# Moving the loads around a gated SSM and linear-attention kernel: a weight's halves on two queues, B in eight quarter loads

## The chip, the cores and the metric

The kernel runs on one core of one Trainium2 chip. The core has five engines that work side by side, each through its own list of instructions in program order: PE (TensorE, the matmuls; its weight loads are shown apart as PEld), DVE (VectorE), ACT (ScalarE), POOL (GpSimd) and SP (SyncE), which computes nothing and issues most of the DMA transfers. The metric is the device time of one execution in microseconds (us); less is better.

## The reference

Everything is bfloat16, S = 2048 rows of D = 512. A state-space branch and a linear-attention branch are mixed by a gate of the row:

```python
g = sigmoid((x * gate_w).sum(-1, keepdims=True))

# branch a: diagonal complex state space, 512 states
dt = exp(log_dt); Lam_bar = exp(dt * Lam)
B_bar = ((Lam_bar - 1) / Lam)[:, None] * (B_re + 1j * B_im)
Bu = einsum("bld,pd->blp", x, B_bar)
h[t] = Lam_bar * h[t-1] + Bu[t]                 # over 2048 steps
a = 2 * einsum("blp,dp->bld", h, C_re + 1j * C_im).real + x * Dskip

# branch b: linear attention, 32 heads of 16
q, k, v = split(x @ wqkv)                       # the input x is A_x
pq, pk = q @ w_phi, k @ w_phi                   # for each head
phi_q = concat(softmax(pq), softmax(-pq));  phi_k = the same of pk
kv = phi_k^T v;  z = sum of phi_k over the rows
o = (phi_q kv) / (phi_q z + 1e-6)
b = o @ wo

out = g * a + (1 - g) * b
```

## The kernel before

The 2048 rows are 16 tiles of 128 rows, x tile 0 to 15, each brought in transposed by one DMA (`x_load`, line 229). The work is cut into stages, Python generators that issue a few instructions and stop at each `yield`. The string `ORDER` (lines 24 to 52) is a list of tokens written out by hand; the loop at line 804 takes each token and moves the stage of that name on by one step. So `ORDER` is the program order of every engine, and of SP's queue too: each engine works off its own part of it, strictly in that order. `@3` names a PSUM bank, `:D` puts an evacuation on DVE in place of ACT, and `F:28` issues 28 filler matmuls on a constant tile.

The stages that the change touches or that follow from it:

- **The key weight.** K's weight (512 x 512, tile `C2r`, line 162) comes in two halves of 256 rows. `W0` to `W3` (line 271) transpose its four row tiles on PE; W0 and W1 read the first half, W2 and W3 the second. `B` (line 342) builds a block diagonal of `w_phi` on DVE from the tile `Wc`. `f0` to `f3` (the folds, line 428) multiply the two on PE and write the folded weight `Wk2`, the evacuations partly on ACT and partly on DVE. `k0` to `k15` (line 478) then multiply an x tile with all of `Wk2`, four matmuls each; `v0` to `v15` do the same with V's weight `Wv`.
- **Small vectors.** POOL loads three vectors of the state space into `vec_n` and two others into `vec_m`. `V` (line 308) transposes `vec_n` on PE and copies it out on DVE; the stages `P`, `P2` and on compute the recurrence's coefficients from it.
- **B.** `NR` and `NI` (line 283) load the real and the imaginary half of B into the tile `Bn`: the real rows in partitions 0 to 63, the imaginary ones in 64 to 127, eight groups of 64 states, t = 0 to 7, along the free dimension. `R0` to `R7` (line 287) transpose one group t of `Bn` into `BT` by DMA. `g` + r + j (line 596) multiplies x with the two groups t = 2j and 2j + 1 of `BT`, four matmuls each, in this order: so g00, g60, g20, g10, g30 and g40 need R0 and R1, g41 is the first that needs R2 and R3, and g23 the first that needs R6.
- **Other DMAs in SP's order.** `l8` to `l15` load x tiles 8 to 15. `C0` to `C7` and `Q0` to `Q3` (lines 295, 291) bring C and Q's weight in transposed; `J0` to `J3` (line 299) rearrange C into the tiles `X1` and `X2`; `O` loads the last weight.

SP's own order before is: `Wc`; x tiles 0 to 3; `Wv`; x tiles 4 to 7; NR; NI; x tiles 10, 13, 9, 12, 14, 11, 8; R0; R1; x tile 15; R2; C4; R3; C6; C3; Q3; Q2; Q1; C7; Q0; C0; R4; C2; R5; C1; C5; six transfers of J; R7; two of J; R6; O. The two halves of K's weight go out on ACT's queue.

The functions that the change touches:

Of the kernel before, what the change touches and what calls it, by code (L numbers as in the profile page):

```python
# [23 lines left out]
ORDER = """
NR F:28 NI B W1@0 W0@1 W0 W2@2 W1:D W3@3 W3 f1@4 W2:D f0@5 f2@6 f0 f1:D l10 V@0 F:4 V P f3@1 f3 f2:D F:4 P P k1@2 k1
l13 P2 k0@3 P2 U P2 P2 P2 P2 P4 k2@4 P3 P3 k3@5 P4 P4 k0 v0@0 i0 i2 U i0 i0 i1 i2 k4@7 i0:D i0 k2 i2 i2:D i2 U k3 k5@6
i1 v3@1 n0 x0 l9 i1 V2@2 i3 l12 x0 k4 v2@3 i3 i3 l14 i1 k5 n0 x0 n0 x0 i3 k7@4 n0 x0 U n0 i1 l11 k6@5 n1 x1 x1 n1 x1
n1 l8 R0 R1 x1 i3 k7 M v7@7 x1 n1 n1 k6:D L V2 v1@6 x2 n2 e0 v6@4 v5@5 v4@2 e0 x2 s0 v0 l15 n2 s0 n2 v2 s0 v1 R2 s0 v6
v3 n2 k10@0 k10 s0 k9@3 k9 C4 k13@6 gw D R3 s0 k12@4 e1 v7 s0 e1 s1 C6 k11@1 k11 x2 s1 k14@0 k8@3 k12 k14 k8 v4 k13
a0@71 a0 x2 s1 x2 s1 v5 g00@4 g00 g60@0 n2 x3 s1 g20@3 g60 s1 g10@2 g10 n3 e2 g30@6 g40@5 g10 s1 a1 x3 g20 n3 a1 x3 n3  # L30
x3 g41@4 n3 C3 e2 e2 e2 x3 g30 g40 g30 k15@0 k15 n3 e3 s2 x4 s2 x4 g01@2 g01 e3 e3 s2 g50@3 g11@5 g50 s2 s2 s2 n4 x4
n4 Q3 n4 s2 g50 g21@6 e3 s3 v8@0 g31@2 g11 Q2 g11 n4 g70@3 Q1 s3 C7 g21 g70 v9@5 g70 g70 z0 z0 g31 g31 Q0 w1@6 C0 a2
a2 a2 w0@3 s3 z0 v11@2 v9 g61@5 g41 R4 z0 w1 v8 z0 z0 g61 s3 w2@4 s3 s3 a2 x4 z0 z0 g51@6 g51 x4 w2 C2 s3 w3@0 g51 v11
n4 R5 w3 g71@5 g71 g71 g71 z1 z1 g02@4 g02 g42@6 a3 a3 z0 z0 g42 w0 e4 e4 z1 z1 z1 g62@2 g12@0 q1@5 C1 h50@4 C5 J1 e4
e4 z1 q2@6 q2 g12 g12 g22@3 g22 J0 h50 z1 z1 g62 q3@4 q3 J2 s4 z1 s4 q0@6 z1 s4 q0 q1 xA nA g32@0 J3 g32 g32 h60@3 J0
g52@2 g52 c4 h60 J2 c4 g52 h51@4 c2 s4 s4 g72@6 R7 g72 xA h10@5 nA g72 g72 c2 xA J3 nA h10 v10@0 v10 J1 s4 c5 h51 c5
R6 g23@3 v12@2 c4 c0 c0 g63@5 nA z2 z2 a3 a3 g03@4 xA g03 z2 z2 z2 z2 xA g23 z2 z2 g33@6 c5 v12 z2 z2 g13@0 g13 g63
g43@4 h32@3 g13 nA g43 h52@2 h52 g33 h32 h61@5 h61 h12@0 c0 g53@4 h12 g33 g53 s4 v14@3 c2 eA eA h42@2 h42 g73@6 g53 eA
eA g73 g73 q10@5 sA h11@0 h11 O h00@4 g73 sA v13@2 h00 v13 a4 z3 sA v15@6 z3 v15 h20@0 h01@4 h30@2 v14 h20 sA h30 z3
h31@6 z3 z3 sA a4 h01 h31 c6 c6 sA q13@3 q13 z3 a4 a4 Y Y h22@0 G q10 z3 z3 G q6@2 q6 h22 z3 z3 sA sA Y Y c1 c1 q9@4  # L40
q8@6 q5@7 h62@3 h41@5 c3 h41 c1 c3 c3 h13@0 h62 q11@2 h13 q11 q8 q12@1 c6 q12 h21@5 q5 h21 h02@2 c7 q4@6 q4 h53@3 h53
h23@1 h23 h33@0 h33 sA q9 h40@7 h40 sA q7@5 h43@6 h63@3 c7 h43 q7 c7 y4@0 y4 sA h63 sA h03@1 END h02 o0@4 o0 X1 N1
o1@7 o1 q14@6 X1 N1 h03 o0@5 X1 o1@2 o1 o1 o0 o0 q15@3 o2@4 o2 o2@7 o2 N1 q15 X1 N1 X1 N1 E1 E1 y2@1 y1@2 y1 E1 E1 q14
X2 y0@5 y0 o1 y4 X2 N2 X2 o0 o0 o3@4 o3 o3@7 o3 o1 o3 y2 X2 N2 o2 X2 N2 S1 S1 N2 S1 o3 S1 N2 S1 S1 o3 y5@3 o2 o2 S1 S1
S1 y1 E2 E2 E2 E2 y9@6 G N3 y5 y5 y3@4 y2 X3 X3 N3 t1 G t1 N3 S1 N3 S2 y9 y9 S2 S2 S1 S1 S2 y3 y3 t3 y0 t0 t0 t2 t2
y6@7 X3 t2:A o4@2 o4 o4@5 o4 o4 y6 y6 t3 X3 o4 X3 o4 S2 S2 t3 o5@1 o5 o5@2 o5 o5 y13@5 y13 o5 N3 o6@4 S2 o6 o6@1 o6 o6
y12@2 o5 y7@4 y7 y12 o6 o6 t4 y7 S2 S2 t4:D S2 E3 E3 E3 E3 S2 o7@1 o7 t5 t5 S3 o7@0 o7 S3 o7 t6 S3 o7 S2 o7 y8@1 o8@3
t6 o8 o8@0 o8 o8 S3 S3 y12 t0:A y11@7 o8 o8 o9@3 o9:D o9@0 o9:D S3 y8 y8 o9 o9 S3 S3 o9 o10@3 y11 o10 o10@0 y11 o10
o10 S3 y14@3 S3 y14 t7 t7:D t8 y14 t8 y15@0 o11@4 S3 o11 o11@1 t9 o12@4 o11:D o11 S3 o10 o10 o12 o12@1 o12 o12 t9:D
o11 y15 o13@4 o13:D o13@6 t6:A o13 o13 o11 o12 y10@1 o14@4 y15 o14:D o12@6 t9 o12:D t7:A t1 y10 y10 o13 o15@4 o15  # L50
o15@6 t4:A t5 o15 o15 t8 o15 t12 t12 t12:A t10 o14@4 o14 o14 t10:D o13@6 t11 o15@2 o15 t10 o13:D t11 t11:A y13 t13 o14
o14@1 t15 t15 t15 o14:D t14 t13 t13 t14 t14:A
"""
# [15 lines left out]
def kernel(  # L69
# [91 lines left out]
    Wv = const.tile([P, KT, D], BF16, name="Wv")  # L161
    wk_nat = const.tile([P, KT, D], BF16, name="C2r")
    C2r = wk_nat
    for k0 in (0, 2):
        nc.scalar.dma_start(out=wk_nat[:, k0:k0 + 2, :], in_=B_wqkv[k0 * P:(k0 + 2) * P, D:2 * D].rearrange("(k p) n -> p k n", p=P))
    nc.sync.dma_start(out=Wc[:], in_=B_w_phi.rearrange("(k hl) e f -> (hl e) k f", hl=8))
# [71 lines left out]
    nc.sync.dma_start(out=Wv[:], in_=B_wqkv[:, 2 * D:3 * D].rearrange("(k p) n -> p k n", p=P))
    for ti in range(4, 8):
        x_load(ti)  # L240
    fk_g = tc.tile_pool(name="featK", bufs=3, reuse_waits="tile")
    fk = fk_g.__enter__()
# [37 lines left out]
        x_load(ti)  # L280
        yield

    def st_N(ri):
        nc.sync.dma_start(out=Bn[ri * 64:(ri + 1) * 64, :, :], in_=(A_B_re, A_B_im)[ri].rearrange("(t p) d -> p t d", p=64))  # L284
        yield

    def st_BT(t):
        nc.sync.dma_start_transpose(out=BT[:, :, t, :], in_=Bn[:, t, :])
# [559 lines left out]
```

## Time and profile before

| what | value |
|---|---|
| time, median of 3 runs | 155.53 us (155.44 to 155.6) |
| span of the profiled execution | 153.2 us |
| busy on PE | 146.2 us, 95% of the span |
| busy on DVE, ACT, POOL | 132.4, 129.2 and 15.8 us |
| DMA | 17.55 MB in 50848 packets, mean 115 GB/s |
| mean granted TensorE clock | 0.99 |

The profile is of one execution. It gives that execution's own time as its span, from its first to its last instruction; the 2.3 us between the span and the median of the runs lie around the instructions that the profile shows. In a row of the timeline stand the start, the duration, the engine, the line of the kernel, the operation and the tiles as written<-read, and the number of instructions merged in the row. "SPq" is a DMA issued by SP: its duration is what the issue takes of SP, not the transfer. A transfer's end is the "landing", told as the time from the start of its issue.

### The profile page before, as it was taken

What the parts mean: (1) busy time and instruction counts of PE and PEld (TensorE: products, weight loads), DVE (VectorE), ACT (ScalarE), POOL (GpSimd) and SP (SyncE); (2) the same over time, 40 slices, a digit from 0 to 9 for tenths busy, and PEclk for the clock granted to TensorE, in tenths of its full rate; (3) what the DMA queues carried; (4) which work ended last, traced back from release to release, by engine and by line L of the source; (5) the groups of instructions that cost most, each with busy time, mean ns of one, the idle gap of its engine ahead of it and who ended that gap; (6) DMA issues with size and microseconds to landing.
All of it is one profiled execution on the core that took longest, in us unless ns stands there. A gap on an engine that the chain in (4) does not pass through costs nothing.

```text
span 153.2 us, 3361 instructions
## 1 busy us (share of the span) xinstructions
PE 146.2 (95%) x1236; PEld 95.0 (62%) x1254; DVE 132.4 (86%) x303; ACT 129.2 (84%) x279; POOL 15.8 (10%) x43
## 2 busy tenths in 40 slices
PE   7899999999999999999999999999999999999990
PEld 7644434788878985869867656555554455555540
DVE  3799999999999999999999999999999958717520
ACT  3489998999998999999998999699498998627562
POOL 8239980000000000000000000000000000000000
PEclk9999999999999999999999999999999999999997
DMA  4875995534445699930000007711278859969842
GB/s 116 164 218 97 223 178 112 103 75 103 103 107 78 129 230 178 166 115 4 0 0 4 0 0 169 74 37 34 42 98 147 176 122 189 162 129 206 247 143 103
DMA packets 50848, 17.55 MB, mean 115 GB/s; under 512 B 44176, under 2 KB 50832, under 8 KB 50832
## 3 DMA queue, kind: packets, MB, share of 16 engines
q1 hardware_dynamic: 48976, 15.75, 53.8%
q10 hardware_dynamic: 1696, 1.57, 3.2%
q8 instruction: 10, 0.16, 0.5%
q0 software_dynamic: 160, 0.01, 0.2%
q14 instruction: 6, 0.05, 0.1%
HBM read 2.64 MB, written 2.10 MB: 31 GB/s over the span
## 4 chain that ended last, share of the span: by engine, by line
PE 78%; SPq 10%; DMA 7%; issue 1%; ACT 1%
PE pgq L601 18%; PE py L717 16%; PE pq L475 9%; PE py L765 8%; SPq L229 8%; PE pv L475 4%; PE ph L668 4%; PE pk L475 4%; DMA xT<-in_A_x_dram 4%; PE kvacc L578 3%; DMA phT<-EEq 3%; PE pn L736 3%; PE pgq L606 2%; PE py L722 2%; PE pgq L608 2%; SPq L284 1%
## 5 line engine op out<-in xcount | busy, mean ns | idle before, releaser
L601 PE MATMUL pgq<-xT,BT 128*128 128x256 bf16 x256 | 31.5, 272 | 0.0
L475 PEld LDWEIGHTS <-xT 128*128 128x128 bf16 x192 | 18.2, 98 | 18.3 <-DMA xT<-in_A_x_dram 0.7
L601 PEld LDWEIGHTS <-BT 128*128 128x128 bf16 x256 | 24.6, 98 | 4.1
L138 ACT ACTIVATE EEk<-EEk 128x1024 bf16<-128x1024 bf16 x20 | 20.4, 1080 | 0.0
L119 ACT CAST uv<-pgq 128x512 bf16<-128x512 f32 x28 | 15.9, 605 | 0.5 <-PE pgq L601 0.4
L475 PE MATMUL pv<-Wv,xT 128*128 128x512 bf16 x59 | 15.5, 379 | 0.3
L475 PE MATMUL pq<-Wq,xT 128*128 128x512 bf16 x60 | 15.4, 379 | 0.2
L765 PE MATMUL py<-Wo,oT 128*128 128x512 bf16 x62 | 15.3, 379 | 0.1
L475 PE MATMUL pk<-Wk,xT 128*128 128x512 bf16 x62 | 14.7, 379 | 0.3 <-DMA xT<-in_A_x_dram 0.2
L138 ACT ACTIVATE EEq<-EEq 128x1024 bf16<-128x1024 bf16 x12 | 11.7, 1042 | 0.3 <-DVE EEq L527 0.3
L769 ACT ACTIVATE ot<-py,G 128x512 bf16<-128x512 f32 x12 | 7.9, 686 | 4.5 <-PE py L765 4.3
L138 ACT ACTIVATE ld<-pn 128x16 f32<-128x16 f32 x32 | 6.1, 191 | 5.7 <-PE pn L736 4.6
L590 ACT ACTIVATE phT<-X,dgB 128x512 bf16<-128x512 bf16 x16 | 10.7, 725 | 0.0
L119 ACT CAST nu<-pn 128x256 bf16<-128x256 f32 x27 | 9.9, 380 | 0.0
L119 ACT CAST vx<-pv 128x512 bf16<-128x512 f32 x16 | 9.1, 604 | 0.4 <-PE pv L475 0.4
L548 DVE TENSOR_TENSOR EEk<-EEk,rck 128x4096 bf16<-128x4096 bf16 (+1 forms) x5 | 9.3, 1858 | 0.0
L744 DVE TENSOR_TENSOR on<-nu,rd 128x512 bf16<-128x512 bf16 x16 | 6.7, 421 | 2.8 <-ACT rd L138 1.6
L765 PEld LDWEIGHTS <-oT 128*128 128x128 bf16 x64 | 5.7, 97 | 5.3 <-DMA oT<-on 0.5
L119 ACT CAST Xq<-pq 128x512 bf16<-128x512 f32 x16 | 8.9, 608 | 0.0
L119 ACT CAST Xq<-pk 128x512 bf16<-128x512 f32 x15 | 8.6, 598 | 0.4 <-PE pk L475 0.4
L736 PEld LDWEIGHTS <-phT 128*128 128x128 bf16 x128 | 6.2, 97 | 3.8 <-DMA phT<-EEq 1.4
L511 DVE TENSOR_TENSOR smk<-smk 128x512 bf16<-128x512 bf16 (+4 forms) x18 | 8.1, 448 | 0.1
(178 smaller groups left out, 321.2 us busy)
## 6 DMA issues: line engine op xcount, KB each, us to landing
X<-HM SPq DMA_DIRECT2D x8, 256.0 KB, 4.5
out_dram<-ot ACTq DMA_DIRECT2D x8, 128.0 KB, 2.5
out_dram<-ot SPq DMA_DIRECT2D x8, 128.0 KB, 2.2
C2r<-in_B_wqkv_dram ACTq DMA_DIRECT2D x2, 256.0 KB, 3.8
Wv<-in_B_wqkv_dram SPq DMA_DIRECT2D x1, 512.0 KB, 4.0
Bn<-in_A_B_re_dram SPq DMA_DIRECT2D x1, 512.0 KB, 5.7
Bn<-in_A_B_im_dram SPq DMA_DIRECT2D x1, 512.0 KB, 6.8
Wo<-in_B_wo_dram SPq DMA_DIRECT2D x1, 512.0 KB, 4.3
```

The source lines that it names most:

```text
L119: nc.scalar.copy(out=out_ap, in_=in_ap)
L138: ins = nc.scalar.activation(**kw)
L229: nc.sync.dma_start_transpose(out=xT[:, :, ti * P:(ti + 1) * P], in_=x_res[ti // 2, ti % 2])
L475: MM(out=pt[:], lhsT=xT[:, kt, ti * P:(ti + 1) * P], rhs=W[:, kt, :], start=(kt == 0), stop=(kt == KT - 1))
L511: VT(out=dst, in0=cur[:, :, :, 0:n, :], in1=cur[:, :, :, n:2 * n, :], op=op)
L548: VT(out=E5, in0=E5, in1=rc.to_broadcast([P, L, 2 * NB, Dh, 4]), op=ALU.mult)
L590: nc.scalar.mul(out=t_, in_=x_, mul=c_)
L601: MM(out=pg[:, h, :], lhsT=BT[:, kt, 2 * j + h, :], rhs=xT[:, kt, r * NC:(r + 1) * NC], start=(h == 0 and kt == 0), stop=(r % 2 == 0 and k ...
L717: MM(out=py[:], lhsT=hs(r, t, slice(a * P, (a + 1) * P)), rhs=C2B[t], start=(t == 0), stop=False)
L736: MM(out=pn[:, 4 * m:4 * m + 4, :].rearrange("p h e -> p (h e)"), lhsT=ph[:, 4 * hf + m, :], rhs=KVm[:, 4 * hf + m, :], start=(m == 0), st ...
L765: MM(out=py[:], lhsT=oT[:, g, :], rhs=Wo[:, g, :], start=False, stop=(g == HG - 1))
L769: nc.scalar.mul(out=ot[:], in_=py[:], mul=G[:, ti:ti + 1])
```

## The change

Four things change, the computation of none:

1. K's weight halves are issued from two queues: the first from ACT as before, the second from SP, where it now stands ahead of `Wc` and the x tiles.
2. V's weight is loaded behind x tile 2 instead of behind x tile 3.
3. B comes in eight loads instead of two. `B0` to `B3` each stand for two groups of t and have two steps, one load of the real and one of the imaginary half (64 partitions x 2 rows of 1 KB, 128 KB). SP's order becomes: second half of K's weight; `Wc`; x tiles 0 to 2; `Wv`; x tiles 3 to 7; x tile 10; B0, B0; x tiles 9, 13, 12, 11, 14, 8; R0; R1; x tile 15; B1, B1; R2; C4; R3; C6; C3; B2, B2; Q3; Q2; Q1; C7; Q0; B3, B3; C0; R4; and from there on as before.
4. On the compute engines, `V` stands behind the fold f3 instead of ahead of it, one of two groups of four filler matmuls there is dropped, k0 stands ahead of k1, and v3 ahead of k4.

The diff, with the parts of `ORDER` left out in which only the line breaks differ:

```diff
 ORDER = """
-NR F:28 NI B W1@0 W0@1 W0 W2@2 W1:D W3@3 W3 f1@4 W2:D f0@5 f2@6 f0 f1:D l10 V@0 F:4 V P f3@1 f3 f2:D F:4 P P k1@2 k1
-l13 P2 k0@3 P2 U P2 P2 P2 P2 P4 k2@4 P3 P3 k3@5 P4 P4 k0 v0@0 i0 i2 U i0 i0 i1 i2 k4@7 i0:D i0 k2 i2 i2:D i2 U k3 k5@6
-i1 v3@1 n0 x0 l9 i1 V2@2 i3 l12 x0 k4 v2@3 i3 i3 l14 i1 k5 n0 x0 n0 x0 i3 k7@4 n0 x0 U n0 i1 l11 k6@5 n1 x1 x1 n1 x1
-n1 l8 R0 R1 x1 i3 k7 M v7@7 x1 n1 n1 k6:D L V2 v1@6 x2 n2 e0 v6@4 v5@5 v4@2 e0 x2 s0 v0 l15 n2 s0 n2 v2 s0 v1 R2 s0 v6
+F:28 B W1@0 W0@1 W0 W2@2 W1:D W3@3 W3 f1@4 W2:D f0@5 f2@6 f0 f1:D l10 B0 B0 f3@1 f3 f2:D V@0 F:4 V P P P k0@2 k0 l9 P2
+k1@3 P2 U P2 P2 P2 P2 P4 k2@4 P3 P3 k3@5 P4 P4 k1 v0@0 i0 i2 U i0 i0 i1 i2 v3@1 k4@7 i0:D i0 k2 i2 i2:D i2 U k3 k5@6
+i1 n0 x0 l13 i1 V2@2 i3 l12 x0 k4 v2@3 i3 i3 l11 i1 k5 n0 x0 n0 x0 i3 k7@4 n0 x0 U n0 i1 l14 k6@5 n1 x1 x1 n1 x1 n1 l8
+R0 R1 x1 i3 k7 M v7@7 x1 n1 n1 k6:D L V2 v1@6 x2 n2 e0 v6@4 v5@5 v4@2 e0 x2 s0 v0 l15 B1 B1 n2 s0 n2 v2 s0 v1 R2 s0 v6
...
+x3 g41@4 n3 C3 B2 B2 e2 e2 e2 x3 g30 g40 g30 k15@0 k15 n3 e3 s2 x4 s2 x4 g01@2 g01 e3 e3 s2 g50@3 g11@5 g50 s2 s2 s2
+n4 x4 n4 Q3 n4 s2 g50 g21@6 e3 s3 v8@0 g31@2 g11 Q2 g11 n4 g70@3 Q1 s3 C7 g21 g70 v9@5 g70 g70 z0 z0 g31 g31 Q0 B3 B3
+w1@6 C0 a2 a2 a2 w0@3 s3 z0 v11@2 v9 g61@5 g41 R4 z0 w1 v8 z0 z0 g61 s3 w2@4 s3 s3 a2 x4 z0 z0 g51@6 g51 x4 w2 C2 s3
...
-    for k0 in (0, 2):
-        nc.scalar.dma_start(out=wk_nat[:, k0:k0 + 2, :], in_=B_wqkv[k0 * P:(k0 + 2) * P, D:2 * D].rearrange("(k p) n -> p k n", p=P))
+    for q_, k0 in ((nc.scalar, 0), (nc.sync, 2)):
+        q_.dma_start(out=wk_nat[:, k0:k0 + 2, :], in_=B_wqkv[k0 * P:(k0 + 2) * P, D:2 * D].rearrange("(k p) n -> p k n", p=P))
...
-    for ti in range(4):
+    for ti in range(3):
         x_load(ti)
     nc.sync.dma_start(out=Wv[:], in_=B_wqkv[:, 2 * D:3 * D].rearrange("(k p) n -> p k n", p=P))
-    for ti in range(4, 8):
+    for ti in range(3, 8):
         x_load(ti)
...
-    def st_N(ri):
-        nc.sync.dma_start(out=Bn[ri * 64:(ri + 1) * 64, :, :], in_=(A_B_re, A_B_im)[ri].rearrange("(t p) d -> p t d", p=64))
-        yield
+    def st_N(q):
+        for ri in range(2):
+            nc.sync.dma_start(out=Bn[ri * 64:(ri + 1) * 64, 2 * q:2 * q + 2, :],
+                              in_=(A_B_re, A_B_im)[ri][2 * q * 64:(2 * q + 2) * 64, :].rearrange("(t p) d -> p t d", p=64))
+            yield
...
     for k in range(4):
+        st[f"B{k}"] = st_N(k)
```

More of the change, by code (lines that the diff above doesn't have):

```diff
@@ L29 @@
+k1@3 P2 U P2 P2 P2 P2 P4 k2@4 P3 P3 k3@5 P4 P4 k1 v0@0 i0 i2 U i0 i0 i1 i2 v3@1 k4@7 i0:D i0 k2 i2 i2:D i2 U k3 k5@6
+i1 n0 x0 l13 i1 V2@2 i3 l12 x0 k4 v2@3 i3 i3 l11 i1 k5 n0 x0 n0 x0 i3 k7@4 n0 x0 U n0 i1 l14 k6@5 n1 x1 x1 n1 x1 n1 l8
+R0 R1 x1 i3 k7 M v7@7 x1 n1 n1 k6:D L V2 v1@6 x2 n2 e0 v6@4 v5@5 v4@2 e0 x2 s0 v0 l15 B1 B1 n2 s0 n2 v2 s0 v1 R2 s0 v6
 v3 n2 k10@0 k10 s0 k9@3 k9 C4 k13@6 gw D R3 s0 k12@4 e1 v7 s0 e1 s1 C6 k11@1 k11 x2 s1 k14@0 k8@3 k12 k14 k8 v4 k13
 a0@71 a0 x2 s1 x2 s1 v5 g00@4 g00 g60@0 n2 x3 s1 g20@3 g60 s1 g10@2 g10 n3 e2 g30@6 g40@5 g10 s1 a1 x3 g20 n3 a1 x3 n3
-x3 g41@4 n3 C3 e2 e2 e2 x3 g30 g40 g30 k15@0 k15 n3 e3 s2 x4 s2 x4 g01@2 g01 e3 e3 s2 g50@3 g11@5 g50 s2 s2 s2 n4 x4
@@ L32 @@
[L32 to L51, printed above, removed]
@@ L52 @@
-o14@1 t15 t15 t15 o14:D t14 t13 t13 t14 t14:A
+x3 g41@4 n3 C3 B2 B2 e2 e2 e2 x3 g30 g40 g30 k15@0 k15 n3 e3 s2 x4 s2 x4 g01@2 g01 e3 e3 s2 g50@3 g11@5 g50 s2 s2 s2
+n4 x4 n4 Q3 n4 s2 g50 g21@6 e3 s3 v8@0 g31@2 g11 Q2 g11 n4 g70@3 Q1 s3 C7 g21 g70 v9@5 g70 g70 z0 z0 g31 g31 Q0 B3 B3
+w1@6 C0 a2 a2 a2 w0@3 s3 z0 v11@2 v9 g61@5 g41 R4 z0 w1 v8 z0 z0 g61 s3 w2@4 s3 s3 a2 x4 z0 z0 g51@6 g51 x4 w2 C2 s3
+w3@0 g51 v11 n4 R5 w3 g71@5 g71 g71 g71 z1 z1 g02@4 g02 g42@6 a3 a3 z0 z0 g42 w0 e4 e4 z1 z1 z1 g62@2 g12@0 q1@5 C1
@@ new lines @@
+h50@4 C5 J1 e4 e4 z1 q2@6 q2 g12 g12 g22@3 g22 J0 h50 z1 z1 g62 q3@4 q3 J2 s4 z1 s4 q0@6 z1 s4 q0 q1 xA nA g32@0 J3
+g32 g32 h60@3 J0 g52@2 g52 c4 h60 J2 c4 g52 h51@4 c2 s4 s4 g72@6 R7 g72 xA h10@5 nA g72 g72 c2 xA J3 nA h10 v10@0 v10
+J1 s4 c5 h51 c5 R6 g23@3 v12@2 c4 c0 c0 g63@5 nA z2 z2 a3 a3 g03@4 xA g03 z2 z2 z2 z2 xA g23 z2 z2 g33@6 c5 v12 z2 z2
+g13@0 g13 g63 g43@4 h32@3 g13 nA g43 h52@2 h52 g33 h32 h61@5 h61 h12@0 c0 g53@4 h12 g33 g53 s4 v14@3 c2 eA eA h42@2
+h42 g73@6 g53 eA eA g73 g73 q10@5 sA h11@0 h11 O h00@4 g73 sA v13@2 h00 v13 a4 z3 sA v15@6 z3 v15 h20@0 h01@4 h30@2
@@ new lines @@
+v14 h20 sA h30 z3 h31@6 z3 z3 sA a4 h01 h31 c6 c6 sA q13@3 q13 z3 a4 a4 Y Y h22@0 G q10 z3 z3 G q6@2 q6 h22 z3 z3 sA
+sA Y Y c1 c1 q9@4 q8@6 q5@7 h62@3 h41@5 c3 h41 c1 c3 c3 h13@0 h62 q11@2 h13 q11 q8 q12@1 c6 q12 h21@5 q5 h21 h02@2 c7
+q4@6 q4 h53@3 h53 h23@1 h23 h33@0 h33 sA q9 h40@7 h40 sA q7@5 h43@6 h63@3 c7 h43 q7 c7 y4@0 y4 sA h63 sA h03@1 END h02
+o0@4 o0 X1 N1 o1@7 o1 q14@6 X1 N1 h03 o0@5 X1 o1@2 o1 o1 o0 o0 q15@3 o2@4 o2 o2@7 o2 N1 q15 X1 N1 X1 N1 E1 E1 y2@1
+y1@2 y1 E1 E1 q14 X2 y0@5 y0 o1 y4 X2 N2 X2 o0 o0 o3@4 o3 o3@7 o3 o1 o3 y2 X2 N2 o2 X2 N2 S1 S1 N2 S1 o3 S1 N2 S1 S1
@@ new lines @@
+o3 y5@3 o2 o2 S1 S1 S1 y1 E2 E2 E2 E2 y9@6 G N3 y5 y5 y3@4 y2 X3 X3 N3 t1 G t1 N3 S1 N3 S2 y9 y9 S2 S2 S1 S1 S2 y3 y3
+t3 y0 t0 t0 t2 t2 y6@7 X3 t2:A o4@2 o4 o4@5 o4 o4 y6 y6 t3 X3 o4 X3 o4 S2 S2 t3 o5@1 o5 o5@2 o5 o5 y13@5 y13 o5 N3
+o6@4 S2 o6 o6@1 o6 o6 y12@2 o5 y7@4 y7 y12 o6 o6 t4 y7 S2 S2 t4:D S2 E3 E3 E3 E3 S2 o7@1 o7 t5 t5 S3 o7@0 o7 S3 o7 t6
+S3 o7 S2 o7 y8@1 o8@3 t6 o8 o8@0 o8 o8 S3 S3 y12 t0:A y11@7 o8 o8 o9@3 o9:D o9@0 o9:D S3 y8 y8 o9 o9 S3 S3 o9 o10@3
+y11 o10 o10@0 y11 o10 o10 S3 y14@3 S3 y14 t7 t7:D t8 y14 t8 y15@0 o11@4 S3 o11 o11@1 t9 o12@4 o11:D o11 S3 o10 o10 o12
@@ L53 @@
+o12@1 o12 o12 t9:D o11 y15 o13@4 o13:D o13@6 t6:A o13 o13 o11 o12 y10@1 o14@4 y15 o14:D o12@6 t9 o12:D t7:A t1 y10 y10
+o13 o15@4 o15 o15@6 t4:A t5 o15 o15 t8 o15 t12 t12 t12:A t10 o14@4 o14 o14 t10:D o13@6 t11 o15@2 o15 t10 o13:D t11
+t11:A y13 t13 o14 o14@1 t15 t15 t15 o14:D t14 t13 t13 t14 t14:A
 """
@@ L778 @@
     st = {"V": st_V(), "V2": st_V2(), "U": st_U(), "P": st_P(), "P2": st_P2(), "P3": st_P3(), "P4": st_P4(), "B": st_B(), "gw": st_gw(),
-          "M": st_M(), "D": st_D(), "L": st_L(), "G": st_G(), "Y": st_Y(), "END": st_END(), "NR": st_N(0), "NI": st_N(1), "O": st_O()}
+          "M": st_M(), "D": st_D(), "L": st_L(), "G": st_G(), "Y": st_Y(), "END": st_END(), "O": st_O()}
     for n in range(8, NTI):
```

## The prediction

> **What bounds the kernel now.** I read the page first, then what PE waits for, then SP's queue in order of time, then the landings of the transfers that the change moves.
>
> ```profile
> span 153.2 us, 3361 instructions
> PE 146.2 (95%) x1236; PEld 95.0 (62%) x1254; DVE 132.4 (86%) x303; ACT 129.2 (84%) x279; POOL 15.8 (10%) x43
> ```
>
> ```profile
> PE pvt L310 <- DMA vec_n<-in_A_log_dt_dram: 0.3, 1, 0.3
> PE ptw L274 <- DMA C2r<-in_B_wqkv_dram: 0.3, 1, 0.3
> PE pk L475 <- DMA xT<-in_A_x_dram: 0.2, 1, 0.2
> ```
>
> PE is busy for 95% of the span. Its waits on transfers add up to 0.8 us, of which the 0.3 of vec_n and the 0.3 of C2r lie ahead of the first key matmul. So PE has almost nothing to win, and each microsecond for which it would have to wait is added to the end. What feeds it is SP's queue:
>
> ```profile
> 0.79 0.45 SPq L166 DMA_DIRECT2D Wc<-in_B_w_phi_dram  x1
> 1.31 5.21 SPq L229 DMA_TRANSPOSE xT<-in_A_x_dram  x4
> 6.57 0.58 SPq L238 DMA_DIRECT2D Wv<-in_B_wqkv_dram  x1
> 7.19 5.12 SPq L229 DMA_TRANSPOSE xT<-in_A_x_dram  x4
> 12.36 1.28 SPq L284 DMA_DIRECT2D Bn<-in_A_B_re_dram  x1
> 13.69 0.62 SPq L284 DMA_DIRECT2D Bn<-in_A_B_im_dram  x1
> 14.36 9.97 SPq L229 DMA_TRANSPOSE xT<-in_A_x_dram  x7
> ...
> 27.00 1.27 SPq L229 DMA_TRANSPOSE xT<-in_A_x_dram  x1
> 28.31 1.26 SPq L288 DMA_TRANSPOSE BT<-Bn  x1
> ...
> 30.92 2.14 SPq L288 DMA_TRANSPOSE BT<-Bn  x1
> ...
> 60.62 2.40 SPq L288 DMA_TRANSPOSE BT<-Bn  x1
> ```
>
> Start plus duration of a row is the start of the next, within 0.1 us: SP issues without a pause, some 1.3 us for each transposing DMA. Whatever is put into this queue moves all that follows it, and so does any wait at its head. How late may it come? R3 (at 30.92) and R6 (at 60.62) are the transposes that stand closest to their reader:
>
> ```profile
> L288 SPq DMA_TRANSPOSE BT<-Bn x1: 2139/2139/2139, 30.9 to 30.9; - x1
> DMA to landing us min/median/max: 3.8/3.8/3.8
> ...
> L288 SPq DMA_TRANSPOSE BT<-Bn x1: 2398/2398/2398, 60.6 to 60.6; - x1
> DMA to landing us min/median/max: 4.3/4.3/4.3
> ```
>
> ```profile
> 35.22 1.03 PE L601 MATMUL pgq<-xT,BT 128*128 128x256 bf16 x8
> ...
> 66.98 1.04 PE L601 MATMUL pgq<-xT,BT 128*128 128x256 bf16 x8
> ```
>
> R3 lands at 30.9 + 3.8 = 34.7. Its reader is g41, whose eight matmuls start at 35.22; the first four read R2, so R3 is due some 0.4 later, at 35.65: slack 0.95. R6 lands at 60.6 + 4.3 = 64.9 and its reader g23 starts at 66.98: slack 2.05. These two numbers decide the change.
>
> **The change part by part.** First the start.
>
> ```profile
> 6.90 0.16 PE L310 MATMUL pvt<-ident,vec_n 12*128 12x12 bf16 x1 [0.29 <-DMA vec_n<-in_A_log_dt_dram]
> 7.22 0.39 PE L431 MATMUL pf<-BD,Xq 128*128 128x128 bf16 x4
> 7.67 3.62 PE L475 MATMUL pk<-Wk,xT 128*128 128x512 bf16 x15
> 11.12 1.03 PE L475 MATMUL pv<-Wv,xT 128*128 128x512 bf16 x4
> ```
>
> *V behind f3, four fillers fewer.* Today f3 starts at 7.22 because V waits for vec_n until 6.90. Behind the other folds f3 fills that wait, and from V at 6.90 only four fillers (0.23, 6.99 to 7.22) lie ahead of k0: it starts at about 7.2, 0.45 earlier. The small-vector work on DVE and ACT then comes behind two evacuations; it is not on PE's path.
>
> *Wv one tile earlier.* k0 to k3 take (11.12 - 7.67)/4 = 0.86 each, so k3 could start at 7.2 + 2.6 = 9.8. But x tile 3 now stands behind Wv, where x tile 4 stands today:
>
> ```profile
> L229 SPq DMA_TRANSPOSE xT<-in_A_x_dram x1: 1198/1198/1198, 7.2 to 7.2; - x1
> DMA to landing us min/median/max: 4.0/4.0/4.0
> ```
>
> SP starts with one more issue of 0.5 (the second half of K's weight, priced below) and has one x tile of 1.3 fewer ahead of Wv, so x tile 3 is issued at 7.2 - 0.8 = 6.4 and lands at 10.4. PE waits for it 0.6; k3 starts at 10.4, where today it starts at 7.67 + 2.6 = 10.25. The gain at the start is spent, and 0.15 more.
>
> *K's halves on two queues.* Both are transferred at once. In the best case the first lands as today and the second, issued 0.5 sooner, as much earlier; in the worst the first lands when the second does today, 0.5 later, which moves k0 to 7.7 at most and is covered by the wait for x tile 3. I take nothing; without that cover it would be 0 to 0.5.
>
> *The two loads of B leave.* From 12.36 to 14.36 SP gains 2.0. One of the x tiles behind them was issued slowly:
>
> ```profile
> L229 SPq DMA_TRANSPOSE xT<-in_A_x_dram x2: 1264/1670/2075, 17.0 to 18.3; - x2
> ```
>
> I count its excess (2.08 - 1.26 = 0.8) as the backlog of that 1 MB, and gone; if not, SP is 0.8 later than below. The x tiles land earlier and PE's wait of 0.2 for one goes, which pays for the 0.15. Up to x tile 15 all is even or better.
>
> *Eight quarter loads.* Their issue isn't in the trace. The nearest rows: 128 rows of 1 KB written out take SP 0.35, 256 rows of 1 KB read take ACT 0.52.
>
> ```profile
> 121.57 0.35 SPq L773 DMA_DIRECT2D out_dram<-ot  x1
> ...
> L165 ACTq DMA_DIRECT2D C2r<-in_B_wqkv_dram x2: 507/518/530, 0.8 to 1.3; - x2
> ```
>
> A quarter has 128 rows and is read: I take 0.46, with the gap to the next 0.5, so 1.0 for a pair (0.8 to 1.1; as slow as the first B load, 1.3 + 0.6 = 1.9).
>
> *The added wait.* Behind x tile 15 SP now has B1, B1, R2. R2 transposes what B1 loads, so it can't be issued before both have landed, and SP issues in order: C4, R3 and all the rest queue behind it. Today R2 starts at 28.31 with B long landed. From the end of an issue to the landing pass:
>
> ```profile
> Wc<-in_B_w_phi_dram SPq DMA_DIRECT2D x1, 16.0 KB, 3.1
> out_dram<-ot SPq DMA_DIRECT2D x8, 128.0 KB, 2.2
> Bn<-in_A_B_im_dram SPq DMA_DIRECT2D x1, 512.0 KB, 6.8
> ```
>
> 3.1 - 0.45 = 2.7 for Wc, 2.2 - 0.35 = 1.85 for a store of the quarter's size, 6.8 - 0.6 = 6.2 for the loads of B that back up. I take 2.7, the small load on the same queue, and keep 1.85 and 6.2 as ends. B0 has seven transposes between it and R0, B2 and B3 several before R4 and R6: no wait there.
>
> [...]
>
> **The sum.** SP's delay when R2 starts: +0.5 (K's half) - 2.0 - 0.8 + 1.0 (B0) + 1.0 (B1) + 2.7 (the wait) = +2.4. R3 lands at 34.7 + 2.4 = 37.1, 1.45 after it is due: PE stands at g41. B2 and B3 add 2.0, so R6 is 4.4 late and lands at 69.3, against 66.98: 2.35 late, of which 1.45 have already passed. PE is 2.35 later in all, and as it has no later wait to give back, so is the end. The profiled execution has a span of 153.2; its median run is 155.53, the 2.3 around the span stay. 155.53 + 2.35 = 157.9.
>
> **The rivals.**
>
> *The loads are cheap.* Pairs at 0.8 and the wait at 1.85: SP is 4.4 - 0.6 - 0.85 = 2.95 late at R6, PE 0.9: 156.4. For it speaks the store's row, against it that both loads in the list take longer.
>
> *The loads back up.* Wait of 6.2: SP is 7.9 late, PE 5.85: 161.4. For it speaks Bn's 6.8; against it that those were 1 MB at once, and a pair here is 256 KB.
>
> *Faster: the earlier keys stay.* The place is the start: k0 0.45 earlier, and the wait of 0.2 for an x tile gone: 154.9. It decides at two points: x tile 3 has to land by 9.8, and R6 may be at most 2.05 - 0.65 = 1.4 late. Without any wait at R2 SP is still 1.7 late there, so it takes a wait near nothing and pairs at 0.8.
>
> *No effect.* Delays stay inside the slack, 0.95 at R3 and 2.05 at R6, and x tile 3 takes what the start gives: 155.5. It needs the wait under 0.4 by my other terms.
>
> **How the numbers follow.** Forecast 0.64, cheap loads 0.14, backing up 0.06, faster 0.11, no effect 0.05. Time 157.9. From 155.6 (no effect) to 159.4 (a wait of some 4.2) leaves out the faster case and most of backing up. Slower by over 0.2%, about what a measurement of this kernel tells from none, are the first three: 0.84; same 0.05; faster 0.11. Within the slower cases alone I expect 156.2 to 159.2.
>
> **What would show it.** In SP's queue: B1's two issues near 27, then a pause of 2 to 3 before R2's transpose, and from there every row 2.4 and later 4.4 behind today's. Among PE's waits: pgq on BT, near 1.5 at g41 and near 0.9 more at g23, and pk on x tile 3, 0.6. k0 near 7.2. A pause at R2 of under 1, or issues of the quarters under 0.3, would make it wrong; so would a g41 and g23 without a wait.

## The result and the profile after

The changed kernel takes 160.16 us (median of 4 runs, 159.46 to 160.63) where the kernel before takes 155.56 (155.44 to 155.69): the ratio is 1.031, with a 95% interval of 1.0277 to 1.0343. It is slower by 4.6 us, where 2.35 were forecast; 160.16 lies 0.8 above the top of the range. Each ratio in this document leaves out disturbed executions, which the medians and ranges keep, and compares with the kernel before as timed in the same round (medians of 155.56 to 155.83).

The page of the changed kernel, first lines:

```profile
span 158.6 us, 3380 instructions
PE 147.9 (93%) x1250; PEld 94.3 (59%) x1250; DVE 132.9 (84%) x303; ACT 130.1 (82%) x279; POOL 13.4 (8%) x43
```

The profiled execution took 160.63, 2.0 more than its span. The span has grown by 5.4 (153.2 before), and PE's busy share has fallen from 95% to 93%: PE still bounds the kernel, but now it waits. What PE waits for in the changed kernel (engine, line, the releaser, its tile; then us in total, times, the longest):

```profile
PE pgq L603 <- DMA BT<-Bn: 2.2, 2, 1.1
...
PE pf L433 <- DVE Xq L121: 0.7, 1, 0.7
PE pn L738 <- DMA phT<-EEq: 0.6, 2, 0.4
PE ptw L274 <- DMA C2r<-in_B_wqkv_dram: 0.5, 1, 0.5
PE py L767 <- DMA oT<-on: 0.4, 1, 0.4
PE pf L433 <- DMA HM<-in_B_wqkv_dram: 0.4, 1, 0.4
PE pv L477 <- DVE Xq L121: 0.4, 1, 0.4
PE kvacc L580 <- DVE EEk L550: 0.3, 1, 0.3
```

The two waits of 2.2 in all on the transposed B are the ones that were forecast. The others are not in the forecast: the start (pf on DVE, and ptw on C2r, which was 0.3 before), the fold of Q's weight (pf on HM), two in the last part (pn on phT, py on oT), and two of 0.4 and 0.3 on DVE (pv, kvacc), with which the lateness of 0.21 at the first keys has become 0.81 at 29 us. SP's queue in order of time shows how the first pair comes about:

```profile
0.79 0.46 SPq L165 DMA_DIRECT2D C2r<-in_B_wqkv_dram  x1
1.31 0.45 SPq L166 DMA_DIRECT2D Wc<-in_B_w_phi_dram  x1
...
15.04 0.74 SPq L285 DMA_DIRECT2D Bn<-in_A_B_re_dram  x1
15.82 0.59 SPq L285 DMA_DIRECT2D Bn<-in_A_B_im_dram  x1
...
28.27 0.60 SPq L285 DMA_DIRECT2D Bn<-in_A_B_re_dram  x1
28.91 0.61 SPq L285 DMA_DIRECT2D Bn<-in_A_B_im_dram  x1
31.77 2.07 SPq L290 DMA_TRANSPOSE BT<-Bn  x1
...
35.18 1.27 SPq L290 DMA_TRANSPOSE BT<-Bn  x1
...
66.47 2.48 SPq L290 DMA_TRANSPOSE BT<-Bn  x1
```

B1's second issue ends at 28.91 + 0.61 = 29.52 and R2 starts at 31.77: SP stands for 2.25, with every transfer of the list behind it. R6 was issued at 60.62 before and is issued at 66.47 now, 5.85 later; it takes 4.3 to land, at 70.8. The answer for the tile `BT` gives R6's landing, and PE's timeline shows its readers and the start:

```profile
L290 SPq DMA_TRANSPOSE BT<-Bn x1: 2476/2476/2476, 66.5 to 66.5; - x1
DMA to landing us min/median/max: 4.3/4.3/4.3
```

```profile
6.53 1.07 PE L433 MATMUL pf<-BD,Xq 128*128 128x128 bf16 x16 [0.66 <-DVE Xq L121]
7.88 3.71 PE L477 MATMUL pk<-Wk,xT 128*128 128x512 bf16 x16
...
37.73 0.61 PE L603 MATMUL pgq<-xT,BT 128*128 128x256 bf16 x4 [1.10 <-DMA BT<-Bn]
...
48.51 0.40 PE L433 MATMUL pf<-BD,HM 128*128 128x128 bf16 x4 [0.37 <-DMA HM<-in_B_wqkv_dram]
...
70.83 1.05 PE L603 MATMUL pgq<-xT,BT 128*128 128x256 bf16 x8 [1.05 <-DMA BT<-Bn]
...
118.71 1.89 PE L767 MATMUL py<-Wo,oT 128*128 128x512 bf16 x8
...
138.88 1.90 PE L767 MATMUL py<-Wo,oT 128*128 128x512 bf16 x8 [0.42 <-DMA oT<-on]
...
152.64 1.89 PE L767 MATMUL py<-Wo,oT 128*128 128x512 bf16 x8
```

The same instructions of the kernel before:

```profile
45.89 0.39 PE L431 MATMUL pf<-BD,HM 128*128 128x128 bf16 x4
...
114.86 1.89 PE L765 MATMUL py<-Wo,oT 128*128 128x512 bf16 x8
...
134.53 1.89 PE L765 MATMUL py<-Wo,oT 128*128 128x512 bf16 x8
...
147.28 1.89 PE L765 MATMUL py<-Wo,oT 128*128 128x512 bf16 x8
```

Put side by side, this is where the time goes: k0 is 0.21 later (7.88 against 7.67), the Q fold 2.62, g23 3.85 (70.83 against 66.98). g23 is set by R6's landing: 5.85 later, less the slack of 2.05 that it had. From there nothing changes until 118.71, still 3.85 later. At 138.88 it is 4.35, at 152.64 it is 5.36. So 3.85 belong to the change's transfers, and 1.5 arise in the last 35 us, on waits for `oT` and `phT`. This is measured against one profile of the kernel before, and an early one: in its two repeats (last experiment) g23 starts at 67.38 and 67.53, so that against them the changed kernel is 3.3 to 3.45 late there. The step from the profiled executions to the medians is small: this one was 0.5 above its median (160.63 against 160.16), and the one profiled before was some 0.3 below (2.3 between span and median there, 2.0 between span and time in each later profile); 5.36 less 0.8 is the 4.6 measured.

### The profile page after: what moved, and what is told of

It reads as the page before. It is cut to its first block, busy times and chain, and to the rows that moved or that the text cites. A ratio compares the mean times of both kernels' runs of the same rounds, so it can differ in the third digit from the quotient of the medians.

```text
span 158.6 us, 3380 instructions
## 1 busy us (share of the span) xinstructions
PE 147.9 (93%) x1250; PEld 94.3 (59%) x1250; DVE 132.9 (84%) x303; ACT 130.1 (82%) x279; POOL 13.4 (8%) x43
## 3 DMA queue, kind: packets, MB, share of 16 engines
q10 hardware_dynamic: 1424, 1.31, 2.7%
```

## The experiments

**Taking away the wait at R2.** In the changed kernel, B1's two loads move ahead of R0, so that three transposing transfers (R0, R1 and x tile 15) lie between them and R2:

```diff
-R0 R1 x1 i3 k7 M v7@7 x1 n1 n1 k6:D L V2 v1@6 x2 n2 e0 v6@4 v5@5 v4@2 e0 x2 s0 v0 l15 B1 B1 n2 s0 n2 v2 s0 v1 R2 s0 v6
+B1 B1 R0 R1 x1 i3 k7 M v7@7 x1 n1 n1 k6:D L V2 v1@6 x2 n2 e0 v6@4 v5@5 v4@2 e0 x2 s0 v0 l15 n2 s0 n2 v2 s0 v1 R2 s0 v6
```

> The changed kernel with its second pair of B loads issued ahead of R0 instead of right ahead of R2. Theory (SP's lateness reaches PE at g41, at the first fold of Q's weight and at g23): R2 no longer waits for its data, its issue starts near 29.6 instead of 31.8, so everything behind it on SP is about 2.2 earlier. The wait of 1.1 at g41 and that of 0.4 at the fold go, the one at g23 shrinks to about 0.8; time about 158.0. Rival (the wait at R2 is no part of it, eight issues in place of two are): R2 and what follows start as late as in the changed kernel, 160.2.

Measured: 158.72 (157.05 to 158.92), ratio 1.0129 (1.0041 to 1.0218). SP's queue in this run:

```profile
24.34 0.60 SPq L285 DMA_DIRECT2D Bn<-in_A_B_re_dram  x1
24.99 0.61 SPq L285 DMA_DIRECT2D Bn<-in_A_B_im_dram  x1
25.64 2.59 SPq L290 DMA_TRANSPOSE BT<-Bn  x2
28.27 1.27 SPq L229 DMA_TRANSPOSE xT<-in_A_x_dram  x1
29.67 1.19 SPq L290 DMA_TRANSPOSE BT<-Bn  x1
```

R2 follows x tile 15 at once. The waits at g41 and at the Q fold are gone, and g23 starts at 68.56 instead of 70.83, after a wait of 0.63. So the pause at R2 is worth 2.27 us at g23; the other 1.58 by which g23 is still late stand with the longer list of issues. The last part of the profiled execution adds 1.9 (waits of 1.6 on `oT`), 0.4 more than in the changed kernel, so that its span is 1.8 shorter.

**B in two loads again.** The changed kernel with the old loads at their old place, all else as changed:

```diff
-F:28 B W1@0 W0@1 W0
+NR F:28 NI B W1@0 W0@1 W0
...
-f0 f1:D l10 B0 B0 f3@1 f3
+f0 f1:D l10 f3@1 f3
...
-s0 v0 l15 B1 B1 n2
+s0 v0 l15 n2
...
-n3 C3 B2 B2 e2
+n3 C3 e2
...
-g31 g31 Q0 B3 B3 w1@6
+g31 g31 Q0 w1@6
```

> The changed kernel with B in the two old loads behind x tile 7; K's halves on two queues, V's weight behind x tile 2 and the small vectors behind f3 stay. Theory: SP is only the one issue of 0.5 later than before at R3 and R6, inside their slack of 0.95 and 2.05, so no wait at g41, at the fold of Q's weight or at g23; what stays is the late start, 0.3 to 0.8 on PE up to g23: 156.2 to 157.0. Rival (the start carries the loss): 159.5 to 160.2.

Measured: 156.68 (155.72 to 157.65), ratio 1.005 (1.0017 to 1.0084). PE waits nowhere on `BT` or on Q's weight; R6 lands at 64.76, and g23 is 0.48 late:

```profile
67.46 0.71 PE L601 MATMUL pgq<-xT,BT 128*128 128x256 bf16 x5
```

Most of the 4.6 us leaves with the quarter loads; what stays is about 0.8. The 0.48 at g23 is no more than what the repeats of the kernel before show (0.40 and 0.55), so it can't be put down to the start.

**The quarter loads alone.** The kernel before with nothing but the eight loads, at the changed kernel's places:

```diff
-NR F:28 NI B W1@0 W0@1 W0
+F:28 B W1@0 W0@1 W0
...
-f0 f1:D l10 V@0 F:4 V
+f0 f1:D l10 B0 B0 V@0 F:4 V
...
-s0 v0 l15 n2
+s0 v0 l15 B1 B1 n2
...
-n3 C3 e2
+n3 C3 B2 B2 e2
...
-g31 g31 Q0 w1@6
+g31 g31 Q0 B3 B3 w1@6
```

> The kernel before with only B's loads changed into the eight quarter loads at the changed kernel's places; K's weight, V's weight, the small vectors and the x tiles as before. Theory: this alone carries the lateness; R6 lands some 5.5 later than before, with 2.05 of slack PE is 3.5 later at g23: 159.0 to 159.5. Rival (the start of the changed kernel carries it: the fold f1 0.9 later, the vector engine behind): 155.6 to 156.5.

Measured: 160.86 (159.07 to 161.31), ratio 1.0278 (1.0196 to 1.036): as slow as the whole change. The pause at R2 is there (B1's second issue at 28.54, R2 at 31.26), and g41 waits 1.0. But then the time goes another way than in the changed kernel. PE's row at Q's fold, SP's issue of the last part of Q's weight (Q0) with its landing, and the stretches around the fold (length; busy us on PE, PEld, DVE, ACT and POOL with the number of instructions, then the granted clock, the DMA share and GB/s):

```profile
49.22 0.40 PE L433 MATMUL pf<-BD,HM 128*128 128x128 bf16 x4 [1.95 <-DMA HM<-in_B_wqkv_dram]
```

```profile
L294 SPq DMA_TRANSPOSE HM<-in_B_wqkv_dram x1: 1258/1258/1258, 44.7 to 44.7; - x1
DMA to landing us min/median/max: 4.4/4.4/4.4
```

```profile
46.70:50.10 3.40, 1.46 (x30) 1.15 (x29) 3.40 (x10) 2.80 (x7) 0.00 (x0) 1.00 0.56 135
50.10:53.40 3.30, 3.08 (x31) 2.07 (x29) 1.31 (x5) 0.63 (x2) 0.00 (x0) 0.50 0.53 109
53.50:56.00 2.50, 2.50 (x36) 2.31 (x35) 1.28 (x2) 1.73 (x4) 0.00 (x0) 1.00 0.36 80
```

PE waits 1.95 for Q's weight. SP's lateness is the smaller part of that: Q0 is issued 0.9 earlier than in the changed kernel (44.75 against 45.65), but takes 4.4 to land, where it takes 2.7 in the kernel before and 2.8 in the changed kernel. Then the granted clock is 0.50 from 50.1 to 53.4. PE is 3.33 late at this fold (49.22 against 45.89) and 4.90 late at the next but one (54.04 against 49.14 before): the stretch at the lower clock costs 1.57. After that R6, which lands at 69.34, is no longer what PE waits for; it was due at 66.98, so R6 alone would have made g23 2.36 late. One execution was profiled, and whether the others had the slow landing and the low clock isn't known, so this run doesn't show that the quarter loads alone cost what the whole change costs. In the 3.40 us before the clock fell PE waited 1.95 us and was busy for 1.46. Shorter waits left the clock at 1.00: 1.10 and 1.05 (g41 and g23 of the changed kernel) and 1.20 (`uv` with R6 moved forward, below). In the executions with waits of 1.43 (`oT` with B1 moved ahead) and 1.52 (g41 with R6 moved forward) the mean clock was 0.994 and 0.997, where it was 0.989 here, and 0.995 in the kernel before, where no wait behind the start is over 0.3.

**K's halves on two queues, alone.**

```diff
-    for k0 in (0, 2):
-        nc.scalar.dma_start(out=wk_nat[:, k0:k0 + 2, :], in_=B_wqkv[k0 * P:(k0 + 2) * P, D:2 * D].rearrange("(k p) n -> p k n", p=P))
+    for q_, k0 in ((nc.scalar, 0), (nc.sync, 2)):
+        q_.dma_start(out=wk_nat[:, k0:k0 + 2, :], in_=B_wqkv[k0 * P:(k0 + 2) * P, D:2 * D].rearrange("(k p) n -> p k n", p=P))
```

> The kernel before with only the second half of K's weight moved to SP's queue, ahead of Wc. Theory: Wc lands about 1.5 later, so the block diagonal and with it the first fold are 0.9 later; the key matmuls, behind V and two groups of fillers, start near 8.3 instead of 7.7; all of SP is 0.5 later, within the slack of R3 and R6. Time about 156.1. Rival (halves on two queues help): key matmuls at 7.2, 155.1. If the first waits on x tiles cover it: 155.6.

Measured: 157.04 (156.06 to 157.8), ratio 1.0059 (1.0023 to 1.0095): slower by little. The first keys start at 8.45 instead of 7.67, and PE is 0.65 late from 36 to 119 us, little more than the two repeats of the kernel before (0.40 and 0.55 at g23). What delays it is not K. `Wc` now stands behind K's second half in SP's queue, and the block diagonal that every fold reads is built from `Wc`. DVE's row in the changed kernel, and in the kernel before:

```profile
5.45 0.69 DVE L345 TENSOR_TENSOR BD<-Wc,mask 128x512 bf16<-128x512 bf16 x1 [2.64 <-DMA Wc<-in_B_w_phi_dram]
```

```profile
3.97 0.69 DVE L343 TENSOR_TENSOR BD<-Wc,mask 128x512 bf16<-128x512 bf16 x1 [1.16 <-DMA Wc<-in_B_w_phi_dram]
```

An issue 0.5 later (1.31 against 0.79) became a landing 1.5 later (5.4 against 3.9). In DVE's program order an evacuation of K's transposed weight queues behind the block diagonal (it starts at 6.06 in the changed kernel, the block diagonal at 5.45), and the first fold waits for that evacuation (the 0.66 on DVE in the changed kernel).

**Wc first.** The changed kernel with `Wc` issued ahead of K's second half:

```diff
+    nc.sync.dma_start(out=Wc[:], in_=B_w_phi.rearrange("(k hl) e f -> (hl e) k f", hl=8))
     for q_, k0 in ((nc.scalar, 0), (nc.sync, 2)):
         q_.dma_start(out=wk_nat[:, k0:k0 + 2, :], in_=B_wqkv[k0 * P:(k0 + 2) * P, D:2 * D].rearrange("(k p) n -> p k n", p=P))
-    nc.sync.dma_start(out=Wc[:], in_=B_w_phi.rearrange("(k hl) e f -> (hl e) k f", hl=8))
```

> The changed kernel with Wc issued ahead of the second half of K's weight on SP. Theory (R6's landing sets the end of the middle, whatever happens ahead of it): the block diagonal is early again, the first fold starts near 5.9 instead of 6.5, but g23 still starts when R6 lands, near 70.8: PE waits longer there, time unchanged at 159.5 to 160.5. Rival (the losses add up): 0.5 to 0.8 less, 159.4 or below.

```profile
5.66 1.24 PE L433 MATMUL pf<-BD,Xq 128*128 128x128 bf16 x16
...
70.50 0.72 PE L603 MATMUL pgq<-xT,BT 128*128 128x256 bf16 x5 [1.17 <-DMA BT<-Bn]
```

The folds start 0.87 earlier, at 5.66, without a wait. Measured: 160.11 (158.68 to 162.26), ratio 1.0242 (1.0178 to 1.0305) where the changed kernel has 1.031 (1.0277 to 1.0343). The intervals overlap, so the times don't tell the theory from its rival; the trace does. g23 is at 70.50 and waits 1.17, because R6 lands at 70.45 whatever the start did; the 0.33 by which it is earlier than in the changed kernel are R6's own. The early loss of the K halves and the late one of the quarter loads are not added: the later of the two arrivals counts.

**V late, alone.** The kernel before with V's transpose behind f3, four fillers fewer and k0 first:

```diff
-f0 f1:D l10 V@0 F:4 V P f3@1 f3 f2:D F:4 P P k1@2 k1
-l13 P2 k0@3 P2 U P2 P2 P2 P2 P4 k2@4 P3 P3 k3@5 P4 P4 k0 v0@0
+f0 f1:D l10 f3@1 f3 f2:D V@0 F:4 V P P P k0@2 k0
+l13 P2 k1@3 P2 U P2 P2 P2 P2 P4 k2@4 P3 P3 k3@5 P4 P4 k1 v0@0
```

> The kernel before with only the small vectors' transpose behind f3, four fillers fewer and k0 ahead of k1. Theory: key matmuls start at 7.2 instead of 7.7, but PE then waits for x tile 9, which still lands near 22.8, so the gain is lost there: 155.4 to 155.6. Rival (the vector engine gets its small vectors later and PE waits for it later on): key matmuls earlier, but waits on vector work of 0.3 to 0.7 near 20 and 29, 155.9 to 156.2. If the start is all that counts: 155.1.

Measured: 155.77 (154.93 to 156.35), ratio 0.9983 (0.9951 to 1.0014): no difference that can be told. The keys do start earlier, at 7.07 against 7.67, and PE keeps 0.35 of the lead until the last part; there the profiled execution loses 1.0.

**Four loads of B.** The kernel before with B in four loads of 256 KB: groups t = 0 to 3 where B stood, 4 to 7 behind C3.

```diff
-NR F:28 NI B W1@0 W0@1 W0
+H0 F:28 H0 B W1@0 W0@1 W0
...
-n3 C3 e2 e2
+n3 C3 H1 H1 e2 e2
...
-        nc.sync.dma_start(out=Bn[ri * 64:(ri + 1) * 64, :, :], in_=(A_B_re, A_B_im)[ri].rearrange("(t p) d -> p t d", p=64))
+            nc.sync.dma_start(out=Bn[ri * 64:(ri + 1) * 64, 4 * q:4 * q + 4, :],
+                              in_=(A_B_re, A_B_im)[ri][4 * q * 64:(4 * q + 4) * 64, :].rearrange("(t p) d -> p t d", p=64))
```

> The kernel before with B in four loads of 256 KB: the groups t = 0 to 3 at the old place, 4 to 7 behind C3, six transposes ahead of R4. Nothing else changes. Theory (late only where SP's lateness passes the slack): no transpose waits for its data; the x tiles land earlier and PE's wait of 0.2 for one goes; R6 is some 0.5 to 1.3 later, inside its slack of 2.05; 155.3 to 155.8, the same within what can be told. Rival (any more issues on SP cost the end their own time, 1.3): 156.8.

Measured: 156.71 (154.62 to 157.92), ratio 1.0012 (0.9974 to 1.005). R6 lands at 64.92 as before, g23 starts at 67.00 (66.98 before), and PE is within 0.02 of the kernel before up to 120 us. Its two added issues (1.3 us of SP) are largely paid for ahead of them: the x tile that was issued slowly before isn't here, and R0 is issued at 23.51 instead of 24.38. So splitting B costs nothing here, where each load stands far ahead of its transpose and the list has only two more issues. What differs lies after 120 us: 1.1 on `oT`, in this execution.

**Four loads with V late.** The last two edits together, the nearest thing to a version that keeps what was good:

```diff
-NR F:28 NI B W1@0 W0@1 W0
+H0 F:28 H0 B W1@0 W0@1 W0
...
-f0 f1:D l10 V@0 F:4 V P f3@1 f3 f2:D F:4 P P k1@2 k1
+f0 f1:D l10 f3@1 f3 f2:D V@0 F:4 V P P P k0@2 k0
...
-n3 C3 e2 e2
+n3 C3 H1 H1 e2 e2
```

> The four loads together with the small vectors' transpose behind f3 (and k0 ahead of k1, four fillers fewer). Theory: key matmuls start at 7.2 or earlier, the x tiles come in time to keep the lead: PE some 0.6 earlier up to g23, 154.9 to 155.3 if the last 30 us follow. Rival (the last part, where PE waits for transposed tiles, gives it back): 155.6 to 156.0.

Measured: 156.29 (155.19 to 156.99), ratio 1.0028 (1.0001 to 1.0055). The keys start at 7.30, but at 28.09 PE has waited 0.35 for DVE's `EEk`, and the lead is 0.13 from there. None of the versions tried is faster than the kernel before.

**R6 moved forward.** If R6's landing sets the loss, bringing it forward should take most of it away. The changed kernel with R6 ahead of six transfers of J:

```diff
-h50@4 C5 J1 e4 e4 z1
+h50@4 C5 R6 J1 e4 e4 z1
...
-J1 s4 c5 h51 c5 R6 g23@3
+J1 s4 c5 h51 c5 g23@3
```

> The changed kernel with R6 issued ahead of the six transfers of J instead of behind the last of them. Theory (g23 starts when R6 lands): R6 lands near 59 to 60, the wait at g23 goes; PE is then 2.6 later than before up to the middle, the part from g41 and the fold of Q's weight, or up to 3.2 where the scaled sums on ACT wait for J's transfers, now 1.3 later still; time 158.9 to 159.6, 0.6 to 1.2 less than the changed kernel. Rival (ACT's wait for J takes the place of R6's): 160.2.

Measured: 162.18 (161.29 to 162.75), ratio 1.0419 (1.0368 to 1.0469): slower still, against my theory's 158.9 to 159.6. R6 lands at 60.09 and g23 no longer waits for it, but J's transfers are now the late ones. ACT's timeline and PE's in this run:

```profile
66.08 0.72 ACT L592 ACTIVATE phT<-X,dgB 128x512 bf16<-128x512 bf16 x1
68.25 0.72 ACT L592 ACTIVATE phT<-X,dgB 128x512 bf16<-128x512 bf16 x1 [1.45 <-DMA X<-HM]
68.88 0.56 ACT L119 CAST uv<-pgq 128x512 bf16<-128x512 f32 x1
```

```profile
69.50 0.27 PE L610 MATMUL pgq<-uv,dg 128*128 128x256 bf16 x1 [1.20 <-ACT uv L119]
```

ACT waits 1.45 for J's tile `X`; the evacuation `uv` queues behind that instruction, and PE waits 1.20 for `uv`. PE is 4.42 late behind it, where R6 had made it 3.85. So R6 is what PE waits for in the changed kernel, but it is only the last of a whole late list: the readers of J are due at nearly the same time. The two profiled executions are 0.6 apart in span, the medians 2.0; what the other executions lost is not shown.

**The kernel before, twice more.** To see what the last part does without any change:

> The kernel before, profiled a second time. If the last 30 us differ from one execution to the next whatever the program, PE is within 0.1 of the first profile up to 115 us, and the waits for transposed tiles behind it are up to 1.5 longer; the span 153.2 to 154.8. If those waits belong to changed programs alone: the span 153.2 within 0.2.

> The kernel before, profiled a third time: the same two cases as for the second, a span between 153.2 and 154.8 if the last part differs by itself, 153.2 within 0.2 if it doesn't.

Spans 153.9 and 154.5 (155.93 and 156.49 us), where the first profile had 153.2. The spans fit the first case, but PE is not within 0.1 of the first profile up to 115 us: at g23 it is 0.40 and 0.55 late already. The waits of the second of them, with one row of its timeline:

```profile
PE py L765 <- DMA oT<-on: 1.0, 1, 1.0
PE pk L475 <- DMA xT<-in_A_x_dram: 0.9, 1, 0.9
```

```profile
135.88 1.47 PE L765 MATMUL py<-Wo,oT 128*128 128x512 bf16 x6 [0.98 <-DMA oT<-on]
```

The same program loses 0.9 on an x tile in both, where the first profile had 0.2, and 1.0 on `oT` at 135.88 in one, where the first profile had none at 134.53. Where the changed kernel is 5.36 late (147.28 before), the repeats are 0.68 and 1.29 late. Differences of half a microsecond between two single profiles, and the last part above all, can't be put down to an edit.

## Why the prediction was right and wrong

**Right: the bound and the mechanism.** PE is the bound, and its lateness at g23 is R6's less the slack of 2.05. B1's loads stop SP's queue for 2.25 (forecast 2.7), g41 waits 1.10 (1.45), g23 1.05 (0.9). That these waits are so close is in part luck: PE itself came 0.81 late to g41, and stood 2.08 behind the kernel before when it went on. With the pause removed 2.27 of the 3.85 at g23 go. "The loads back up" would have needed a pause of 6.2, "the loads are cheap" one of 1.85 and issues of 0.4; neither is in the rows. (The sum of "the loads are cheap" took 0.6 off for its pairs; four pairs at 0.8 instead of 1.0 are 0.8, and its time is 156.2.) "No effect" and "faster" fell with the pause.

**Wrong: the sum of SP's delay at R6, 4.4 forecast and 5.85 measured.** By its terms, forecast and measured: K's half +0.5 and +0.5; the two loads of B that leave -2.0 and -2.0; the slow issue of x tile 12 -0.8 and -0.8, with a slow issue of x tile 10 that was not forecast, +0.85; B0 +1.0 and +1.4; B1 +1.0 and +1.25; the pause +2.7 and +2.25; B2 and B3 +2.0 and +2.5. The measured terms add up to 5.95, within 0.1 of the queue's 5.85. Two of them carry the error:

- *The price of a quarter's issue.* I put it between a store of 128 rows (0.35) and a load of 256 rows (0.52), at 0.46. It is 0.60, and 0.74 for the first behind the x tiles. The row for it stood in the list: the second of B's own loads, 512 rows into the same 64 partitions, took 0.62. SP's other loads of 256 and 512 rows take 0.46 and 0.58, so in these loads the number of rows hardly mattered, and the store was the wrong neighbour. Eight times 0.15 is 1.2.
- *The slow x tile.* "I count its excess as the backlog of that 1 MB, and gone" was right of x tile 12 and wrong of the queue. The answers for the x tiles' issues (min/median/max in ns, first and last start), in the changed kernel from 11 to 15 us and with four loads of B from 10 to 24 us:

```profile
L229 SPq DMA_TRANSPOSE xT<-in_A_x_dram x2: 1266/1692/2119, 11.6 to 12.9; - x2
```

```profile
L229 SPq DMA_TRANSPOSE xT<-in_A_x_dram x9: 1259/1265/1301, 9.8 to 22.2; - x9
```

With only half a megabyte issued at once no x tile is slow in this run. With the two old loads the kernel before has an x tile of 2.08 at 18.3 us in its first profile and one of 2.35 between 14.5 and 22.5 in its first repeat; the changed kernel's six x tiles from 16.5 to 24.3 take 1.26 to 1.29: in these profiles x tile 12's excess goes with the 1 MB. But in the changed kernel x tile 10, at 12.9, takes 2.12 with no load of B near it, where before B's first load had the excess at that time (1.28 where its twin took 0.62). R0 is issued at 24.41 against 24.38: the time stayed, on another transfer.

With 5.85 in place of 4.4 the same working (5.85 less 2.05 of slack) gives 3.8, and 159.3 us: the 3.85 that g23 shows. The 0.8 from there to the measured 160.16 are the next point.

**Wrong: "it has no later wait to give back, so is the end".** That PE gives nothing back is true: 3.85 stands from 70.83 to 118.71. But the last part adds 1.5 in the profiled execution. I had looked for slack there and not asked what has none: before, the tile `oT` lands at 134.46 and is read at 134.53, and PE already waits 0.2 for `phT` there, which my list of PE's waits left out. The run of four loads, which is even with the kernel before up to 120 us, loses 1.2 there too, and one of the repeats of the kernel before loses on the same tile. So the last part can lose this without any change to SP's list; how much of the 1.5 is the change's stays open.

**Wrong, and covered: the start.** "K's halves on two queues ... I take nothing" weighed K and not what stands behind it: `Wc` lands 1.5 later, f1 waits 0.66 and k0 starts at 7.88, not 7.2. The wait of 0.6 for x tile 3, forecast to absorb the gain, never came, since the keys were late themselves (it landed at 10.50, forecast 10.4). Alone this edit costs 0.6% (K's halves alone); within the change it costs little, because R6 lands later than PE could come anyway (the run with `Wc` first).

**Not on my list:** the fold of Q's weight waits, 0.37 in the changed kernel and 1.95 with the quarter loads alone. I had taken R3 and R6 for the two transposes nearest to their reader among those of B, and did not ask the same of the other transfers behind R2: Q0 lands at 43.6 before, 2.25 ahead of its fold, about as close as R6. In the profile of quarters alone this wait, with a slow landing and the low clock behind it, set the loss instead of R6.

**The pause.** The list of DMA issues of the changed kernel has, for a quarter, from the start of its issue to its landing:

```profile
Bn<-in_A_B_re_dram SPq DMA_DIRECT2D x4, 128.0 KB, 3.1
```

Of these 3.1, 0.6 are the issue, and the pause of SP's queue was 2.25. The term of 2.7 from the row of `Wc` was 0.45 too long, the 1.85 from the row of the stores 0.4 too short.

## What to carry to other kernels

Where a queue issues transfer after transfer without a gap, list for every transfer behind the edit, and not only for the ones the edit names, how long before its reader it lands; the delay at each reader is the delay of the queue less that slack (5.85 less 2.05 at g23 here, with 3.85 measured), and several delays on one path combine as the latest arrival, not as a sum (with `Wc` first the folds came 0.87 earlier, g23 0.33). The load put directly ahead of its own consumer stopped SP's whole queue here, for 2.25 us, and the same load three transposes earlier did not: R2's issue followed x tile 15's within 0.13 us. Price a small transfer by its issue, which was nearly the same for 128 KB as for 512 KB (0.60 and 0.62): cutting two loads into eight added six issues and no speed, cutting them into four cost nothing that could be measured.
